# Linformer attention and a gated FFN: k' of batch 1 transposed by TensorE instead of by a DMA

## The chip, the cores and the metric

The kernel runs on one core of a Trainium2 chip. The metric is the device time of one execution in microseconds (us); of several runs the median is given. The core's engines are TensorE (PE in the profile; PEld are its weight loads), VectorE (DVE), ScalarE (ACT), GpSimd (POOL) and SyncE (SP). Each takes its instructions in the order in which the program issues them and waits on semaphores for the others. TensorE writes into PSUM, which has eight banks; VectorE and ScalarE read it from there.

## What is computed

Attention with projected keys and values (8 batches, 8 heads, 1024 positions, 64 features a head; E and F project the 1024 positions to 64), and behind it an FFN with a gelu:

```
k_proj = einsum('ks,bhsd->bhkd', E, k)
v_proj = einsum('ks,bhsd->bhkd', F, v)
scores = (q @ k_proj^T) / sqrt(64)
attn   = softmax(scores)
x      = attn @ v_proj            # to (8192 tokens, 512)
h      = x @ w_in                 # 512 -> 2048
out    = (h * sigmoid(1.702 h)) @ w_out   # 2048 -> 512
```

Below, k' and v' are `k_proj` and `v_proj`. For the scores, TensorE needs k' with the head's features on the partitions, that is, transposed from the form in which the projections leave it.

## The kernel before

**Blocks and slots.** The 8192 tokens are worked off in 16 blocks of 512, two to a batch. Block j needs its attention output `xT[j]`; then come the first FFN matmul (`ffn1`, L421) in slots 0 to 15, one slot for each 128 of the 2048 features (four matmuls with 512 columns and one gelu on ScalarE, L427 and L429), and the second FFN matmul. From block 1 on the second matmul is done in the manner of Strassen, as seven products named 1 to 7, each in two halves (L534), whose operands are sums of pieces of `gT` (the gelus' output) and of `w_out`, made by VectorE (`g_sum`, L508; `w_sums`, L465 and L469).

**What fills the slots.** The order of the instructions is written out by hand. `at(j, slot, ...)` puts further work behind a slot of block j, in the order of the calls; slots from O = 16 on are the halves of the seven products. In block 1 stand the following, all of them for the next batches:

- slot 1: SyncE's DMA transposes of the first half of q of batch 1 (`q_dma`, L264); slot 12: the second half
- slot 5: the projections of k and v of batch 1 (`proj`, L184), 16 matmuls into one PSUM bank, and `kv_out`: VectorE copies k' to `k_b` (L232), SyncE transposes it by DMA into `kts[1]` (L233), and VectorE copies v' into `vx1` and `vqs[1]` (L225, L226)
- slot 6: the last two operations of `w_sums` on VectorE
- slots 7, 13 and 15, ahead of what `at` puts there: the four sums of `g_sum` each, over four, three and one chunk of features
- slot O + 1, behind product 1: the scores of block 2 (`scores`, L274), which read `kts[1]` and the first half of q, and their exponentials on ScalarE (L293), for which ScalarE loads another table first; slots O + 3 and on: the values (`tok`, L399) and their transposes (`x_tr`, L414); slot O + 9: the scores of block 3

The k' of the other batches takes two ways. That of batch 0 is transposed by TensorE in three pieces: `k_piece` calls `k_tr` (L203), which transposes against an identity into PSUM (L207) and has VectorE copy the result into `kts[0]` (L209). That of batches 2 to 7 goes by DMA (L233 and L784).

**PSUM banks.** Each of the eight banks is one buffer: whoever takes it next waits until the last reader of the one before is done. Until the slots of block 1 end (`opening`), `f_tile` deals out banks 0 to 3 in turn, afterwards banks 0 to 4:

```
f_next[0] += 1
return bank(f_next[0] % (4 if opening[0] else 5), shape, dt)
```

In block 1 the projections of batch 1 are the 57th taker (bank 1), slots 6, 7 and 8 take banks 2, 3 and 0, slot 9 bank 1 again, slots 10 to 12 banks 2, 3 and 0. The scores, the values, the projections of batch 2 and the slots of block 2 go on with the count, now over five banks; slot 15 of block 2 is the 109th taker. From there the count is no longer used: the rest is a list of steps with banks named by hand (L598), which begins with the products of block 2 (L661), while scores and exponentials of the next blocks are mixed in (L741 and L740):

```
BANK = dict(FD=0, FB=4, FG=0, A0=6, A1=1, B0=7, B1=3, G0=2, G1=5, S10=5, S11=7, V00=4, V01=0,
            S00=3, S01=2, V10=6, V11=5, D0=2, D1=5, PJ=1)
AHEAD = {
    (2, None):
        "F1.0@2 F1.1@2 Fc1@2 sc.1@4 sc.0@4 ex.1.0@4 ex.1.1@4 F2.0@2 ex.0.0@4 ex.0.1@4 F2.1@2 sc.1@5 "
```

F1.0 and F1.1 are the halves of product 1 of block 2, into bank FD; Fc1 copies it on ScalarE into bank FB (L643); `sc` and `ex` are scores and exponentials.

Of the kernel before, what the change touches and what calls it, by code (L numbers as in the profile page):

```python
# [18 lines left out]
def kernel(ctx, tc, q, k, v, E, F,  # L19
                                                     moe_w_in, moe_w_out, out):  # L20
    nc = tc.nc
# [91 lines left out]
    kts = [consts.tile([P, HP, KP], BF16, name=f"kt{i}") for i in range(2)]  # L113
# [25 lines left out]
    def f_tile(shape, dt=F32):  # L139
        f_next[0] += 1  # L140
        return bank(f_next[0] % (4 if opening[0] else 5), shape, dt)
# [18 lines left out]
    for i, cp in enumerate((nc.vector.tensor_copy, nc.scalar.copy)):  # L160
        t_ps = f_tile([P, J // 2, 2 * KP], BF16)
# [10 lines left out]
    def eft(j, cols=slice(0, 2 * KP)):  # L172
        return efts[j // (J // 2)][:, j % (J // 2), cols]
# [4 lines left out]
    def proj(b):  # L178
        def go():
            if b not in kvps:  # L180
                kvps[b] = f_tile([P, H, D])
            for j in range(J):
                for e, r in enumerate((LO, HI)):
                    nc.tensor.matmul(kvps[b][r], eft(j, slice(e * KP, (e + 1) * KP)),  # L184
                                     (kt, vt)[e][b][:, :, j, :],
                                     start=(j == 0), stop=(j == J - 1))
        return go
# [8 lines left out]
    def k_piece(h0, n):  # L196
        k_ps = proj0(0, h0, n)
        k_b = att.tile([KP, n, D], BF16, name=f"k0_b{h0}", bufs=1)
        nc.vector.tensor_copy(k_b, k_ps[LO])
        warm(2)  # L200
        k_tr(k_b, h0 // 2)

    def k_tr(k_b, p0):  # L203
        n = k_b.shape[1] // 2
        t_ps = f_tile([P, n, KP], BF16)
        for p in range(n):
            nc.tensor.transpose(t_ps[:, p, :], k_b[:, 2 * p:2 * p + 2, :].rearrange("k t d -> k (t d)"),  # L207
                                ident[:KP, :KP])
        nc.vector.tensor_copy(kts[0][:, p0:p0 + n, :], t_ps)  # L209

    def vx_of(b, p):
        return vx1[:, 2 * p:2 * p + 2] if b == 1 else vx0[p]
# [7 lines left out]
    def v_out(b, v_ps):  # L220
        vv = v_ps[HI].rearrange("k (u x) d -> k u x d", x=4)
        for r, xs_ in ((LO, X_LO), (HI, X_HI)):
            if b == 1:
                vx = vx1[r, :, :D].rearrange("k (u x) d -> k u x d", x=4)
                nc.vector.tensor_copy(vx[:, :, xs_], vv[:, :, xs_])  # L225
            nc.vector.tensor_copy(vqs[b % 2][r].rearrange("k (u e) d -> k u e d", e=2), vv[:, :, xs_, :])  # L226

    def kv_out(b, cp=nc.vector.tensor_copy):
        def go():
            ps = kvps.pop(b)  # L230
            k_b = att.tile([KP, H, D], BF16, name="k_b")
            cp(k_b, ps[LO])  # L232
            nc.sync.dma_start_transpose(out=kts[b % 2], in_=k_b.rearrange("k h d -> k (h d)"))  # L233
            v_out(b, ps)
        return go

    q0s = [[early[:, (4 + 2 * g + u) * TB:(5 + 2 * g + u) * TB].rearrange("p (j i s) -> p j i s", j=2, i=2)
            for u in range(2)] for g in range(2)]
# [21 lines left out]
    def q_dma(b, j0=0, n=J):  # L260
        def go():
            if j0 == 0:
                qT[b] = att.tile([P, J, HP, P], BF16, name="qT")
            nc.sync.dma_start_transpose(out=qT[b][:, j0:j0 + n].rearrange("r j p s -> r (j p) s"),  # L264
                                        in_=qt[b][:, j0:j0 + n].rearrange("s j h d -> s (j h d)"))
        return go
# [542 lines left out]
    def at(j, slot, *fs):  # L809
        fill.setdefault((j, slot), []).extend(fs)  # L810
# [44 lines left out]
    for p in range(HP):  # L855
        at(0, Q + (4, 6, 9, 11)[p], tok(1, p, 0), tok(1, p, 1))
        at(0, Q + (6, 9, 11, 12)[p], x_tr(1, p, 0), x_tr(1, p, 1))
    at(1, 1, q_dma(1, 0, JB))
    at(1, 5, proj(1), kv_out(1))
    at(1, 12, q_dma(1, JB, JB))  # L860
    for u in range(2):
        at(1, O + 1, scores(2, u))
# [7 lines left out]
    at(1, O + 6, q_dma(2))  # L870
    at(2, 3, spread(3, nc.gpsimd), lambda: load(3))
    at(2, 1, proj(2), kv_out(2, nc.scalar.copy))
    for i, f in enumerate(w_in_sums()):
        at(2, (4, 6, 8, 10, 15, 15)[i], f)
# [49 lines left out]
    for j in range(2, 14):  # L924
        ahead(j, None)
        for word in STEPS:
            m = word.replace("-", "+-").split("+")
            name, n = m[0], j + int(m[1] if len(m) > 1 else 0)
# [3 lines left out]
    for word in END:  # L932
        name, n, swap, banks = re.fullmatch(r"(.*)@(\d+)(!?):?(.*)", word).groups()
# [32 lines left out]
```

## Time and profile before

| | |
|---|---|
| median of 3 runs | 476.46 us (476.27 to 476.97) |
| the profiled execution | 476.55 us, of it the span of the profile 474.7 us |
| TensorE busy | 464.2 us, 98% of the span |
| VectorE, ScalarE busy | 317.1 us, 320.1 us (67% each) |
| GpSimd busy | 83.2 us (18%) |
| TensorE's granted clock | 1.00 in every part of the span |
| slots 0 to 15 of block 1 | up to 68.68 us |
| scores of block 2 | from 72.46 us |
| products of block 2 | from 103.52 us |

The span is what the profile covers; the rest of the time lies before and behind it. A row of the timeline gives the start and the length in us, the engine, the line of the kernel, the operation, the tile written and the tile read, their sizes, how many instructions are taken together, and in brackets how long the engine stood idle before it and what ended that. In the chain of waits, followed back from the end of the program, each piece gives a start, a length and what it was; "SPq" is SyncE issuing transfers, "issue" the time in which nothing was waited for that the profile shows.

### The profile page before, as it was taken

To read this page: it belongs to the slowest core of one execution; us is meant where nothing else is said; L and a number is where in the kernel's file an instruction comes from. 1 tells how busy PE (TensorE), PEld (TensorE's weight loads), DVE (VectorE), ACT (ScalarE), POOL (GpSimd) and SP (SyncE) were. 2 spreads that over 40 slices of the span, in tenths; PEclk is the share of its full clock that TensorE was granted. 3 is DMA by queue.
4 is the path that set the end of the run, shared out by engine and by line. 5 is a ranking of instruction groups with operands and counts; after the bars stand their busy time and mean duration, and the time that the engine had idled before them with its cause. 6 is when DMAs were issued, how large, how long until landed. Compare 5 with 4: busy or idle time off the path is not lost.

```text
span 474.7 us, 10490 instructions
## 1 busy us (share of the span) xinstructions
PE 464.2 (98%) x4331; PEld 356.7 (75%) x4331; DVE 317.1 (67%) x589; ACT 320.1 (67%) x556; POOL 83.2 (18%) x104
## 2 busy tenths in 40 slices
PE   8999998998999999999999999999999999999996
PEld 4644446555778788787888878787888878888885
DVE  4503895399495775858587675867768585859472
ACT  2665455566596787967687886857788695848561
POOL 7562161062032100501041010500000000000000
PEclk9999999999999999999999999999999999999999
DMA  9999999979999999945999389942280413412022
GB/s 169 200 188 206 228 169 146 253 145 188 124 202 211 205 179 212 169 92 140 215 217 128 116 130 217 193 92 97 61 210 9 105 70 91 155 27 88 1 90 90
DMA packets 132963, 69.19 MB, mean 146 GB/s; under 512 B 98340, under 2 KB 122420, under 8 KB 132916
## 3 DMA queue, kind: packets, MB, share of 16 engines
q0 software_dynamic: 86816, 30.43, 58.1%
q1 hardware_dynamic: 46020, 37.84, 32.7%
q8 instruction: 34, 0.56, 0.5%
q10 hardware_dynamic: 80, 0.26, 0.2%
q14 instruction: 13, 0.11, 0.1%
HBM read 72.88 MB, written 16.99 MB: 189 GB/s over the span
## 4 chain that ended last, share of the span: by engine, by line
PE 81%; DMA 13%; DVE 2%; POOL 1%; SPq 1%; ACT 1%; issue 1%; DVEq 0%; POOLq 0%; ACTq 0%
PE k_ps L661 35%; PE k_ps L712 34%; DMA q_sb<-in_q_dram 4%; PE k_ps L274 3%; PE k_ps L427 3%; DMA w_in_sb<-in_moe_w_in_dram 2%; PE k_ps L184 2%; DMA w_out_sb<-in_moe_w_out_dram 2%; PE k_ps L534 2%; DMA v_sb<-in_v_dram 2%; DMA kt<-k_b 2%; SPq L264 1%; PE k_ps L754 1%; DVE xT L748 1%; POOL k_sb L59 0%
## 5 line engine op out<-in xcount | busy, mean ns | idle before, releaser
L646 DVE TENSOR_TENSOR q_even<-k_ps,q_even 128x512 f32<-128x512 f32 x104 | 70.3, 688 | 55.2 <-PE k_ps L712 54.0
L661 PEld LDWEIGHTS <-sg 128*128 128x128 bf16 x896 | 87.3, 98 | 11.8 <-issue 1.8
L712 PEld LDWEIGHTS <-late 128*128 128x128 bf16 x832 | 80.4, 98 | 12.7 <-PE k_ps L661 2.3
L712 PE MATMUL k_ps<-xw,late 128*128 128x256 bf16 x624 | 89.3, 273 | 0.6 <-DVE xw L500 0.6
L661 PE MATMUL k_ps<-tw,sg 128*128 128x256 bf16 x672 | 82.5, 273 | 0.3 <-DVE u_sb L643 0.3
L728 ACT ACTIVATE gT<-k_ps 128x512 bf16<-128x512 f32 x104 | 62.3, 600 | 27.0 <-PE k_ps L712 25.4
L661 PEld LDWEIGHTS <-gT 128*128 128x128 bf16 x672 | 65.8, 98 | 8.3 <-issue 0.4
L712 PEld LDWEIGHTS <-w_in_sb 128*128 128x128 bf16 x624 | 58.3, 98 | 17.7 <-issue 10.8
L728 ACT ACTIVATE gT<-q_even 128x512 bf16<-128x512 f32 x104 | 61.4, 630 | 4.4 <-DVE q_even L646 4.3
L712 PE MATMUL k_ps<-xT,w_in_sb 128*128 128x256 bf16 x416 | 62.3, 273 | 1.0 <-ACT vq L643 1.0
L643 ACT COPY q_even<-k_ps 128x512 f32<-128x512 f32 x63 | 36.0, 590 | 38.8 <-PE k_ps L712 38.0
L71 POOL DMA_DIRECT2D q_sb<-in_q_dram x48 | 42.1, 904 | 105.3 <-DMA qT<-q_sb 68.6
L661 PE MATMUL k_ps<-w_out_sb,gT 128*128 128x256 bf16 x448 | 55.6, 273 | 0.1
L427 PE MATMUL k_ps<-xT,w_in_sb 128*128 128x512 bf16 (+1 forms) x200 | 42.7, 371 | 0.0
L508 DVE TENSOR_TENSOR sg<-gT 128x1024 bf16<-128x1024 bf16 (+2 forms) x64 | 41.4, 647 | 0.0
L429 ACT ACTIVATE gT<-k_ps 128x512 bf16<-128x512 f32 (+1 forms) x50 | 28.9, 580 | 17.9 <-PE k_ps L427 17.7
L427 PEld LDWEIGHTS <-w_in_sb 128*128 128x128 bf16 x200 | 19.3, 98 | 21.3 <-issue 0.8
L748 DVE TENSOR_TENSOR xT<-k_ps,rbc 128x512 bf16<-128x512 f32 x52 | 33.5, 679 | 0.0
L643 DVE COPY q_even<-k_ps 128x512 f32<-128x512 f32 x41 | 27.1, 684 | 8.7 <-PE k_ps L712 8.7
L716 ACT COPY k_ps<-k_ps 128x512 f32<-128x512 f32 x52 | 29.3, 588 | 3.2 <-DVE xT L748 1.2
L712 PE MATMUL k_ps<-xw,w_in_sb 128*128 128x256 bf16 x208 | 31.2, 273 | 0.0
L712 PE MATMUL k_ps<-xT,late 128*128 128x256 bf16 x208 | 31.0, 273 | 0.0
(134 smaller groups left out, 541.0 us busy)
## 6 DMA issues: line engine op xcount, KB each, us to landing
out_dram<-o_sb SPq DMA_DIRECT2D x31, 512.0 KB
rbc<-rdr SPq DMA_DIRECT2D x24, 512.0 KB
k_sb<-in_k_dram POOLq DMA_DIRECT2D x7, 1024.0 KB, 10.4
v_sb<-in_v_dram POOLq DMA_DIRECT2D x7, 1024.0 KB, 16.2
q_sb<-in_q_dram POOLq DMA_DIRECT2D x48, 128.0 KB, 6.0
w_in_sb<-in_moe_w_in_dram POOLq DMA_DIRECT2D x8, 256.0 KB, 11.4
w_out_sb<-in_moe_w_out_dram POOLq DMA_DIRECT2D x4, 512.0 KB, 11.5
q_even<-in_q_dram POOLq DMA_DIRECT2D x12, 128.0 KB, 14.8
```

Source lines behind the costliest of these rows:

```text
L71: nc.gpsimd.dma_start(out=qt[b][:, j], in_=qv[:, j])
L274: nc.tensor.matmul(outs[i][r.start + c:r.start + c + w], lhsTs[i][ri, c:c + w], rhss[i][ri], start=True, stop=True)
L427: nc.tensor.matmul(h_ps, w_in_sb[:, kc, fc * P:(fc + 1) * P], xT[j][:, kc, ts], start=(kc == 0), stop=(kc == KC - 1))
L429: nc.scalar.activation(gts[j][:, fc, ts], h_ps, AF.Gelu_apprx_sigmoid)
L508: nc.vector.tensor_tensor(t[i - 1], in0, in1, op=ALU.add if i == 1 else ALU.subtract)
L643: (nc.scalar.copy if (n in ON_ACT) != swap else nc.vector.tensor_copy)(out_, in_)
L646: nc.vector.tensor_tensor(out_, in0, in1, op=ALU.add)
L661: nc.tensor.matmul(at_(n)[:, 0 if one else t], x[:, c, t * P:(t + 1) * P], w[:, c], start=(i in (1, 5) and (one or t == 0) and c == 0), st ...
L712: nc.tensor.matmul(at_(h)[:, r], a[:, c, f:f + P], w[:, c], start=(i in (1, 5) and r == 0 and c == 0), stop=(i in (2, 3, 4) and r == 1 and ...
L716: nc.scalar.copy(new(f"B{m}", [P, 2, TH], f"B{n}"), at_(f"A{n}"))
L728: nc.scalar.activation(out_, in_, AF.Gelu_apprx_sigmoid)
L748: nc.vector.tensor_tensor(x_of(j)[:, u, :], at_(f"V{p[1]}{t}"), rbc[j][:, u, :], op=ALU.mult)
```

## The change

k' of batch 1 is no longer transposed by SyncE's DMA but by TensorE. `kv_out` keeps `k_b` of batch 1 in a list in place of issuing the DMA transpose; `k_tr` is given the batch, and is called behind slot 8 of block 1, three features' chunks behind the projections. It takes one bank of the ring, issues four transposes on TensorE and one copy of 128x256 on VectorE into `kts[1]`. The k' of batch 0 and of batches 2 to 7 goes as before.

```diff
-    def k_tr(k_b, p0):
+    def k_tr(k_b, p0, b=0):
         n = k_b.shape[1] // 2
         t_ps = f_tile([P, n, KP], BF16)
         for p in range(n):
             nc.tensor.transpose(t_ps[:, p, :], k_b[:, 2 * p:2 * p + 2, :].rearrange("k t d -> k (t d)"),
                                 ident[:KP, :KP])
-        nc.vector.tensor_copy(kts[0][:, p0:p0 + n, :], t_ps)
+        nc.vector.tensor_copy(kts[b][:, p0:p0 + n, :], t_ps)
...
             k_b = att.tile([KP, H, D], BF16, name="k_b")
             cp(k_b, ps[LO])
-            nc.sync.dma_start_transpose(out=kts[b % 2], in_=k_b.rearrange("k h d -> k (h d)"))
+            if b == 1:
+                k_bs.append(k_b)
+            else:
+                nc.sync.dma_start_transpose(out=kts[b % 2], in_=k_b.rearrange("k h d -> k (h d)"))
             v_out(b, ps)
         return go
+
+    k_bs = []
...
     at(1, 5, proj(1), kv_out(1))
+    at(1, 8, lambda: k_tr(k_bs[0], 0, 1))
     at(1, 12, q_dma(1, JB, JB))
```

## The prediction

> **What bounds the kernel now.** I read the page first, then the chain of waits in order of time around the change, then the timeline there engine by engine, last the waits of the later stretches. TensorE is busy for 98% of the span; time can only be won or lost where it stands still. From 116 us on it is busy for 352.46 of 354 us, and no transfer is in the chain after 72.46 us. What is gained or lost at 60 to 75 us, where this change lies, therefore reaches the end unless something between 75 and 116 us swallows it.
>
> The chain of waits there (start, us, what):
>
> ```profile
> 63.15 9.27 DMA kt<-k_b
> 72.42 0.04 issue
> 72.46 0.62 PE k_ps L274 x16
> 73.08 1.85 PE k_ps L534 x16
> 74.94 0.23 PE k_ps L399 x4
> ```
>
> k' of batch 1 is ready in SBUF at 60.85 us, but SyncE issues the transposes of q's first half until 63.10, and the transposed k' lands 9.27 us after its own issue begins. TensorE has finished the part before (L534) at 70.81 us and stands for 1.65 us until the scores (L274) may start. That is all that the change can remove.
>
> The timeline of VectorE in the same place, with the one TensorE weight load that had to wait, and below it four rows of ScalarE (start, us, engine, line; in brackets the idle time before and what ended it):
>
> ```profile
> 60.17 0.68 DVE L232 CAST k_b<-k_ps 64x512 bf16<-64x512 f32 x1 [2.83 <-PE k_ps L184]
> ...
> 62.02 0.42 DVE L226 CAST vq<-k_ps 64x256 bf16<-64x256 f32 x1
> 62.47 2.29 DVE L465 TENSOR_TENSOR tw<-w_out_sb,rbc 128x2048 bf16<-128x2048 bf16 x1
> 62.49 0.68 PEld L427 LDWEIGHTS <-w_in_sb 128*128 128x128 bf16 x4 [0.18 <-DVE vq L226]
> 64.68 1.22 DVE L469 CAST tw<-rbc 128x2048 bf16<-128x2048 f32 x1
> 65.81 0.68 DVE L508 TENSOR_TENSOR sg<-gT 128x1024 bf16<-128x1024 bf16 x1
> ...
> 67.74 0.68 DVE L508 TENSOR_TENSOR sg<-gT,sg 128x1024 bf16<-128x1024 bf16 x1
> 68.34 0.55 DVE L508 TENSOR_TENSOR sg<-gT 128x768 bf16<-128x768 bf16 x1
> 67.22 0.60 ACT L429 ACTIVATE gT<-k_ps 128x512 bf16<-128x512 f32 x1 [0.33 <-PE k_ps L427]
> 70.89 0.57 ACT L565 COPY k_ps<-k_ps 128x512 f32<-128x512 f32 x1 [1.35 <-PE k_ps L534]
> 71.48 1.28 ACT L293 ACT_TABLE_LOAD   x1
> 72.91 0.60 ACT L293 ACTIVATE expT<-k_ps 128x512 bf16<-128x512 f32 x1
> ```
>
> Two things are to be seen. VectorE has no gap from 60.17 to 71.35 us. And the weight load at 62.49, the first of slot 9, waited for vq (L226), the last reader of the projections' bank: four PSUM banks go round in this stage, and slot 9 is the fourth taker after the projections.
>
> **The change, part by part.**
>
> *Removed:* one transpose issue on SyncE (1.30 us at 63.15) and its 9.27 us in flight, and with them TensorE's 1.65 us. On SyncE the second half of q's transposes is next (issued 64.61 to 72.36); it could begin up to 1.5 us earlier if its q has landed. Its readers, the scores of block 3, start at 81.68 and waited for VectorE, not for it: nothing.
>
> *Added on TensorE:* four transposes 64x128 to 128x64 behind slot 8. The same operation for batch 0 (L207) has 199 ns each by its own record; a pair there holds the next weight load up from 9.68 to 9.84, 0.08 us each. Four cost 0.32 us by that (0.16 at half, 0.80 at full records). Their inputs are there: k_b since 60.85, and the bank, which is now the projections' own, since 62.44, just as slot 9 had it.
>
> *Added on VectorE:* one copy 128x256 bf16 out of PSUM. L415 copies exactly that in 282 ns (278 to 292).
>
> *The new wait.* The transposes' result takes the fourth turn of the ring, where slot 9 was. Slots 9, 10 and 11 take the other three; slot 12 comes round to the transposes' bank and must wait until VectorE has copied it. VectorE's order is the program's: behind the projections' copies stand the two w_out sums put at slot 6 (L465 2.29, L469 1.22) and the four gT sums of slot 7 (L508), and only then the copy of slot 8. So the copy starts where now the slot-13 sum starts, 68.34, and ends at 68.62; 0.05 us later, as from vq to the load at 62.49, slot 12 starts at 68.67. Bounds of this: 68.55 if the copy overlaps its predecessor more, 68.85 if it waits for the 68.42 end and takes 0.35.
>
> Before, slots 12 to 15 (16 matmuls of 0.216) ended at 68.68, so slot 12 began at 65.22. **It is 3.45 us late** (3.3 to 3.65). In the new kernel TensorE would have come to slot 12 at 62.64 + 0.32 + 3 x 0.865 = 65.55, so it idles 3.1 us there, and the four transposes cost nothing: this wait hides them. By the Trainium skill, "TensorE: Matmul & The Clock Gate", Part 4, a transpose takes some 390 ns alone for 128x128; four such would put TensorE at 66.8 in place of 65.55, still before 68.67, and the sum would be the same.
>
> Behind slot 12 on TensorE's queue stand slots 13 to 15, part 1 of the second matmul and the scores. VectorE's later gT sums wait for their gelu and move along: the slot-13 sum starts at 71.4 (its gelu, 67.22 + 0.60, plus 3.45), the slot-15 sums end at 74.4; what part 5 reads of them is done by 73.7, and part 5 starts at 74.9. Nothing.
>
> *What is won back.* Part 1 ends at 70.81 + 3.45 = 74.26. k' (68.62) and the first half of q are there, so the scores follow at once. But ScalarE's path then ends last: from the end of part 1 it takes 0.08 to L565, 0.57 for it, 0.02, 1.28 for the table load, 0.02, 0.60 for the first exponential and some 0.04 to TensorE, 2.61 in all, against 0.03 + 0.62 + 1.85 = 2.50 on TensorE. The values (L399) start at 74.26 + 2.61 = 76.87 in place of 74.94. Of the 1.65 us, 1.5 are won.
>
> That makes + 3.45 - 1.52 = + 1.93 us (1.75 to 2.2) at 77 us.
>
> *A second wait, from the count of banks.* The transposes take one turn more of the ring, and every later turn falls one bank further. Within the ring this changes nothing, for the distances stay. (Where four banks become five, the scores meet the bank of block 1's slot 15, whose gelu ends at 73.0, before 74.26.) But block 2 goes over from the ring to banks named by hand. Its slot 15 is the 109th taker: 109 mod 5 is bank 4, and bank 0 is slot 11's. With one more it is the 110th: bank 0, the bank named FD, into which the very next TensorE work, product 1 of block 2 (L661), writes. So that must wait until slot 15's gelu has been read out of it:
>
> ```profile
> 103.55 0.60 ACT L429 ACTIVATE gT<-k_ps 128x512 bf16<-128x512 f32 x1 [0.27 <-PE k_ps L427]
> 105.34 0.57 ACT L643 COPY k_ps<-k_ps 128x512 f32<-128x512 f32 x1 [1.19 <-PE k_ps L661]
> ...
> 111.16 0.69 DVE L643 COPY u_sb<-k_ps 128x512 f32<-128x512 f32 x1 [0.47 <-PE k_ps L661]
> ```
>
> Slot 15's gelu ends at 104.15; the chain has L661 begin at 103.52. With 0.05 to TensorE it begins at 104.20: **0.68 us late** (0.63 by the release alone; 0.85 if the weight load, now fetched ahead at 103.14, is paid as well). Nothing covers it: the copy at 105.34 waits for L661, and behind it on ScalarE stand the table load and the exponentials that the chain follows up to 111 us. The other named banks (4, 3, 2 and 1) fall to slots 14, 13, 12 and 11, whose gelus are done before they are needed.
>
> *Does it last?* VectorE's run of work from 94.81 on hangs on a gather issued by SyncE behind q's transposes of batch 2, which wait for a load; it may stay in place while TensorE is later. But at 111.16 VectorE was already waiting 0.47 us for TensorE, so a later TensorE only lengthens that: nothing is swallowed.
>
> **Sum:** + 1.93 + 0.68 = **+ 2.6 us** (2.35 to 3.05). Profiled execution: span 474.7, 476.55 in all; with the change 479.15. The median of the runs lies 0.09 below it: 476.46 + 2.6 = **479.1**.
>
> **The rivals.**
>
> *A, the copy holds nobody up (not slower).* If slot 12 found its bank free, part 1 would end at 70.81 + 0.32 and the values start at 71.13 + 2.61 = 73.74, 1.2 us earlier; with 0.68 lost at 103.5, 0.5 is left, and VectorE's 0.47 us of waiting at 111.16 lets through no more if its work from 94.81 on stays where it is: 476.0. For it: for batch 0 the copies (L209) follow their transposes within 0.3 us. Against: VectorE is idle before those, and full here. It decides if the copy gets past the sums. Chance 0.04.
>
> *B, the change frees nothing: q is the late one.* The first half of q's transposes shares SyncE's queue with k', and the scores could be waiting for it all along; with a free slot 12 the time would be 476.5 + 0.7 = 477.1. Against: the chain names k', issued after it, and in my forecast TensorE comes at 74.26, after both. 0.04.
>
> *C, one of the waits is missing or is partly swallowed.* TensorE idles 0.89 us in 103 to 116; if that closed, or if the second wait did not come about, 0.7 to 0.9 less: 478.2 to 478.4. For it: much there hangs on VectorE, busy for 12.46 of those 13 us. Against: its waits follow TensorE's own work. 0.10.
>
> *D, the clock drops in the gap.* TensorE's longest gap in mid-kernel is now 1.65 us, and the granted clock is 1.00 in every stretch; the new gap is 3.1 us. The records do show a slower TensorE: at 5.04, 5.46 and 5.89 us the loads of the 128x512 warm matmuls follow each other in 0.43 us, where later ones take 0.216. Were the 16 matmuls of slots 12 to 15 run so, 16 x 0.21 = 3.4 more: 482.5; half of them, 480.8. It decides from the point at which a gap is long enough to count. 0.10. The same page of the skill, Part 1, has the clock halved after an idle window of some 3.4 us; by that length 3.1 us is just too short and the sum stays, and no row here shows such a gap yet. Its closing table warns of gaps above about 3 us, and by that D would be the case.
>
> **How the numbers follow.** Forecast 0.72, its own range 478.6 to 479.8 (the sum's bounds, and 0.3 us of spread: the runs before lie from 476.27 to 476.97). A to D take 0.28. The range 478.0 to 480.8 takes in C and D's lower half; it leaves out A, B, D's upper half and some of the tails, under 2 in 10. A measurement of this kernel can tell 0.2%, 0.95 us, from no change: faster is under 475.5 (a tail of A, 0.02), same up to 477.4 (A, B: 0.07), slower the rest, 0.91.
>
> **What would show it.** Right: slot 12's weight load idle some 3 us with VectorE's new copy (line 209) as releaser; that copy starting at about 68.3, straight after the fourth L508; no wait of L274 for a transfer; the values at 76.9; L661 waiting some 0.6 us for ScalarE's gelu at about 106. Wrong: the copy near 63 us (A); L274 waiting for qT (B); no wait of L661 for the gelu, or less lateness at 116 us than at 106 (C); matmuls of 0.4 us after the gap (D).

## The result, and the profile after

The changed kernel takes 481.41 us (median of 4 runs, 479.85 to 483.79) against 476.50 us before: a ratio of 1.0106, 95% interval 1.0064 to 1.0148. It is slower, as forecast, but by 4.9 us where 2.6 were forecast, and outside the range. The profiled execution took 481.41 us, with a span of 479.6 us.

Line numbers from L234 on are higher by five in the changed kernel (L427 is L432, L508 L513, L534 L539, L661 L666, L274 L279), and by six in some of the experiments from their own edit on.

The place of the first wait, from the timelines of VectorE and TensorE in the changed kernel:

```profile
68.00 0.68 DVE L513 TENSOR_TENSOR sg<-gT,sg 128x1024 bf16<-128x1024 bf16 x1
68.72 0.29 DVE L209 COPY kt<-k_ps 128x256 bf16<-128x256 bf16 x1
73.32 0.56 DVE L513 TENSOR_TENSOR sg<-gT 128x768 bf16<-128x768 bf16 x1 [4.32 <-ACT gT L434]
62.99 0.29 PE L207 MATMUL k_ps<-ident,k_b 64*128 64x64 bf16 x4
63.21 2.76 PE L432 MATMUL k_ps<-xT,w_in_sb 128*128 128x512 bf16 x12
69.06 5.30 PE L432 MATMUL k_ps<-xT,w_in_sb 128*128 128x512 bf16 x16 [3.09 <-DVE kt L209]
```

The copy of k' comes straight after the fourth gT sum, and slot 12 waits 3.09 us for it. What had not been put into the sum stands in the last row: the 16 matmuls of slots 12 to 15 take 5.30 us in place of the 3.46 (16 x 0.216) of the kernel before. The windows of the changed kernel show a lower clock there (the stretch, its length, busy time of PE, PEld, DVE, ACT and POOL with their instructions, then the granted clock, the DMA share and GB/s):

```profile
66.00:69.00 3.00, 0.00 (x0) 0.00 (x0) 2.93 (x6) 0.60 (x1) 2.39 (x3) 1.00 1.15 169
69.00:72.00 3.00, 2.94 (x8) 1.04 (x8) 0.01 (x1) 0.60 (x1) 0.00 (x0) 0.52 1.28 182
72.00:75.00 3.00, 3.00 (x17) 1.58 (x16) 1.64 (x4) 1.74 (x3) 0.89 (x1) 0.91 2.00 128
```

In the three us after the gap only eight matmuls ran, at a granted clock of 0.52. Before the change that clock is 1.00 throughout.

The place of the second wait, in the chain of waits of the kernel before and then of the changed one:

```profile
91.32 12.19 PE k_ps L427 x56
103.52 1.76 PE k_ps L661 x16
```

```profile
107.73 0.61 ACT gT L434
108.34 0.04 issue
108.38 1.92 PE k_ps L666 x16
110.30 0.03 ACTq L648
```

Product 1 of block 2 now follows slot 15's gelu; before, it followed slot 15's matmuls. The lateness against the kernel before changes from stage to stage as follows (starts in us, from the chains and timelines of the two profiled executions; slot 12 before is 68.68 less 16 matmuls of 0.216):

| | before | after | later by |
|---|---|---|---|
| copy of k' to `k_b`, ahead of all that was changed | 60.17 | 60.43 | 0.26 |
| slot 12 | 65.22 | 69.06 | 3.84 |
| ScalarE's copy behind part 1 (L565, L570) | 70.89 | 76.40 | 5.51 |
| values (L399, L404) | 74.94 | 78.94 | 4.00 |
| second part behind them (L534, L539) | 75.16 | 79.34 | 4.18 |
| product 1 of block 2 (L661, L666) | 103.52 | 108.38 | 4.86 |
| ScalarE's copy behind it (L643, L648) | 105.34 | 110.37 | 5.03 |
| end of the span | 474.7 | 479.6 | 4.9 |

The first 0.26 us is the opening, the work ahead of all that was changed. This copy of k' starts at 60.17 in the one profile of the kernel before and at 60.38 to 61.02 in the twelve others of this case; whether the change has a part in that isn't shown. The rest is: first wait + 3.58, slow matmuls + 1.67, won back at the scores - 1.51, second wait + 0.68, and twice a group behind a wait that takes longer, the values + 0.18 (0.40 us in place of 0.23 in the chain) and product 1 + 0.17 (1.92 in place of 1.76). This longer time behind a wait is called the refilling of TensorE's pipeline below; the name is a reading, the times are measured. (The chain of the changed kernel names VectorE's sums ahead of ScalarE's copy L570. The copy starts at 76.40, 0.08 us after part 1 ends on TensorE, at 76.32; before, it was 70.89 after 70.81, the same 0.08. So it still follows TensorE.)

### The profile page after: what moved, and what is told of

Read it like the earlier page. It is cut to its first block, busy times and chain, and to the rows that moved or that the text cites. A ratio compares the mean times of both kernels' runs of the same rounds, so it can differ in the third digit from the quotient of the medians.

```text
span 479.6 us, 10488 instructions
## 1 busy us (share of the span) xinstructions
PE 465.5 (97%) x4327; PEld 356.7 (74%) x4335; DVE 317.8 (66%) x590; ACT 319.9 (67%) x556; POOL 83.2 (17%) x104
## 4 chain that ended last, share of the span: by engine, by line
PE 89%; DVE 4%; DMA 3%; ACT 2%; POOL 1%; issue 1%; DVEq 0%; ACTq 0%; POOLq 0%
PE k_ps L666 35%; PE k_ps L717 34%; PE k_ps L432 8%; PE k_ps L279 3%; PE k_ps L444 3%; PE k_ps L184 3%; DMA v_sb<-in_v_dram 3%; PE k_ps L539 2%; DVE sg L513 1%; PE k_ps L759 1%; DVE xT L753 1%; DVE tw L470 0%; POOL k_sb L59 0%; POOL v_sb L59 0%; PE k_ps L404 0%
## 5 line engine op out<-in xcount | busy, mean ns | idle before, releaser
L666 PEld LDWEIGHTS <-sg 128*128 128x128 bf16 x896 | 87.3, 98 | 11.8 <-issue 1.8
L666 PE MATMUL k_ps<-tw,sg 128*128 128x256 bf16 x672 | 82.5, 273 | 0.3 <-DVE u_sb L648 0.3
L666 PEld LDWEIGHTS <-gT 128*128 128x128 bf16 x672 | 65.7, 98 | 9.2 <-issue 1.4
L648 ACT COPY q_even<-k_ps 128x512 f32<-128x512 f32 x63 | 36.0, 590 | 38.9 <-PE k_ps L717 38.1
L666 PE MATMUL k_ps<-w_out_sb,gT 128*128 128x256 bf16 x448 | 55.6, 273 | 0.8 <-ACT gT L434 0.7
L432 PE MATMUL k_ps<-xT,w_in_sb 128*128 128x512 bf16 (+1 forms) x195 | 44.4, 381 | 3.4 <-DVE kt L209 3.1
L513 DVE TENSOR_TENSOR sg<-gT 128x1024 bf16<-128x1024 bf16 (+2 forms) x64 | 41.5, 648 | 6.1 <-ACT gT L434 6.1
L432 PEld LDWEIGHTS <-w_in_sb 128*128 128x128 bf16 x200 | 19.6, 100 | 25.7 <-issue 6.4
L648 DVE COPY q_even<-k_ps 128x512 f32<-128x512 f32 x41 | 27.1, 685 | 8.7 <-PE k_ps L717 8.7
```

What stands on the lines that cost most here:

```text
L432: nc.tensor.matmul(h_ps, w_in_sb[:, kc, fc * P:(fc + 1) * P], xT[j][:, kc, ts], start=(kc == 0), stop=(kc == KC - 1))
L513: nc.vector.tensor_tensor(t[i - 1], in0, in1, op=ALU.add if i == 1 else ALU.subtract)
L648: (nc.scalar.copy if (n in ON_ACT) != swap else nc.vector.tensor_copy)(out_, in_)
L666: nc.tensor.matmul(at_(n)[:, 0 if one else t], x[:, c, t * P:(t + 1) * P], w[:, c], start=(i in (1, 5) and (one or t == 0) and c == 0), st ...
```

## The experiments

The theory: two waits on banks, each of the size above, and on top of them a clock that drops in the 3.1 us gap in most executions. Against it stood that the slow matmuls have another cause, that the second wait is hidden, and that the transposes on TensorE cost by themselves.

**Work in the gap.**

```diff
     at(1, 8, lambda: k_tr(k_bs[0], 0, 1))
+    at(1, 11, lambda: warm(14))
```

> The changed kernel with 14 matmuls of zeros (128x512, 0.216 us each, into a bank that is free) behind slot 11, so that TensorE works through most of the 3.1 us in which it waits for VectorE's copy of k'. Theory 'bank waits and clock' (3.1 us of idleness lower the clock, the 16 matmuls of slots 12 to 15 then take 5.35 us in place of 3.46): the clock stays at 1.00 in every execution, slots 12 to 15 take 3.5 us, and the time is 476.5 + 2.3 (first wait, net) + 0.84 (second wait) = 479.6, all runs within 0.5 us of each other. Rival 'the slow matmuls have another cause' (refilling of TensorE's queue, the transfers running at that time): slots 12 to 15 still take over 5 us and the time is some 481.4.

479.93 us (six runs, 479.85 to 480.18; ratio 1.0058, 1.0039 to 1.0077). Its timeline of TensorE:

```profile
66.25 3.19 PE L152 MATMUL k_ps<-zeros 128*128 128x512 bf16 x14
69.50 3.61 PE L432 MATMUL k_ps<-xT,w_in_sb 128*128 128x512 bf16 x15
```

Slots 12 to 15 start just as late after the transposes as in the changed kernel (6.06 us against 6.07), but they take 3.61 us in place of 5.30 (one record is missing of the 16), at a clock of 0.998 or more in every run. TensorE did 14 matmuls more and the kernel became 1.5 us faster. The loss behind the gap is the clock, and the gap's idleness is its cause: only the idleness was taken away, and the loss went with it.

**The result in a bank outside the ring,** which takes both waits away and leaves the change otherwise as it is:

```diff
-        t_ps = f_tile([P, n, KP], BF16)
+        t_ps = (x_any if b else f_tile)([P, n, KP], BF16)
```

> The changed kernel with the transposes' result put into a bank outside the ring (bank 7, which has no other user until product 5 of block 1). Theory 'bank waits and clock': VectorE's copy stays where it is, at about 68.7, but nobody on TensorE waits for it; slot 12 starts at once, no clock drop, no wait of L666 for the gelu at 104; the scores follow part 1 at 71.1 and the values start at 73.8, 1.2 us earlier than before the change. By VectorE's 0.47 us of waiting at 111 us only that much is left at the end: 476.0 (475.3 if all of it passes). Rival 'q is the late one': the scores wait for q's transposes at 72.4 and the time is 476.5 or more. Rival 'transposes on TensorE cost more than 0.3 us': 476.5 to 477.5.

> The changed kernel with the transposes' result in a bank outside the ring, once more, beside the next one: 476.0, 0.5 to 0.8 below the kernel before the change.

476.00 us (12 runs; before, on the same chip, 476.67; ratio 0.9983, 0.9971 to 0.9996), and the second time 475.85 (before 476.46; ratio 0.9995, 0.9983 to 1.0008). There is no wait for k' and none for the gelu, and the scores follow part 1 at once, as these rows of TensorE show:

```profile
63.22 6.22 PE L432 MATMUL k_ps<-xT,w_in_sb 128*128 128x512 bf16 x28
71.33 0.62 PE L279 MATMUL k_ps<-qT,kt 64*32 64x512 bf16 x16
74.01 0.40 PE L404 MATMUL k_ps<-vx,expT 128*128 128x130 bf16 x4 [0.21 <-ACT expT L298]
```

So rival B of the prediction, by which the scores wait for q, is out. The time is the 476.0 of rival A, but that is a coincidence: A had the second wait in it, and this kernel has none. In the chain of the first of these runs the stretch from 88.7 to 111 us no longer goes through TensorE:

```profile
88.74 1.82 SPq L269
90.56 0.05 issue
90.61 0.58 SPq L547
91.19 0.05 issue
91.24 0.02 SPq L328
91.26 0.04 issue
91.29 3.52 DMA rc<-den
94.81 0.02 issue
94.83 0.07 DVE rc L337
...
109.58 1.09 DVE late L496
110.67 0.08 issue
110.75 0.05 DVE u_sb L648
```

The gather waits on SyncE behind the transposes of q of batch 2, which stand where they stood, and VectorE's work behind it ends at 110.67, as before. So of the 1.2 us that the change is worth at the values (74.01 against 74.94, with an opening 0.26 us later), 0.6 to 0.7 came to the end by the medians; the interval of the second ratio takes in 1.

**The same, with the ring's count put forward by one,** so that the second wait alone is there:

```diff
             opening[0] = False
+            f_next[0] += 1
```

> As the run with the bank outside the ring, but with the ring's count put forward by one behind block 1, as in the changed kernel, so that slot 15 of block 2 takes bank 0 again. Theory 'bank waits and clock': L666 waits for slot 15's gelu as in the changed kernel (0.7 us idle and 0.16 for filling TensorE's pipeline again); the time is 0.84 above the run without it if that passes in full, 0.4 above it if VectorE's backlog had eaten the gain already. Rival 'the second wait is hidden': equal times.

476.88 us (12 runs; ratio to before 0.9999, 0.9987 to 1.0010), 0.88 above the run without the count on the same chip. The list of TensorE's waits (us in total, times, longest) has the one for the gelu again:

```profile
PE k_ps L666 <- ACT gT L434: 0.7, 1, 0.7
```

The second wait passes in full, and it alone takes away all that the change had to give. This, not the kernel without the count, is the case of rival A, and A had 476.0 for it. It carried the whole 1.2 us on to product 1; of them 0.87 are left there (102.91 without the count, 103.52 before, the opening taken off), and the second wait takes 0.68 and 0.17 more for the refilled pipeline.

**The changed kernel with only the second wait taken away:**

```diff
             opening[0] = False
+            f_next[0] += 4
```

> The changed kernel with the ring's count put forward by four more behind block 1, so that block 2 has the banks of the kernel before the change; the first wait stays. Theory 'bank waits and clock': no wait of L666 for the gelu; the time is 0.84 below the changed kernel's: 480.6 where the clock drops (a granted clock of 0.5 for 3.4 us or less), 479.0 where it doesn't, and so a spread of one to two us between the runs as the changed kernel has it. Rival 'the second wait is hidden': 481.4.

480.65 us (six runs, 479.03 to 482.05; ratio 1.0076, 1.0053 to 1.0099), 0.76 below the changed kernel. Among executions with the same clock it is 0.8 below (table further down): 479.03 against 479.84 and 479.85 at full clock, 480.61 against 481.45 by the medians of the middle group. The wait for the gelu is gone, the one for k' is there. Its profiled execution, the slowest of the six:

```profile
69.39 6.45 PE L432 MATMUL k_ps<-xT,w_in_sb 128*128 128x512 bf16 x16 [3.08 <-DVE kt L209]
```

The same gap as in the changed kernel, and all 16 matmuls slow.

**A shorter and a longer gap.** The first puts one of VectorE's sums behind the copy, the second does it twice more ahead of the copy:

```diff
-        at(*((0, Q + 10), (0, Q + 13), (0, Q + 13), (0, Q + 13), (1, 6), (1, 6))[i], f)
+        at(*((0, Q + 10), (0, Q + 13), (0, Q + 13), (0, Q + 13), (1, 6), (1, 9))[i], f)
```

```diff
+    at(1, 8, w_sums[5], w_sums[5])
     at(1, 8, lambda: k_tr(k_bs[0], 0, 1))
```

> The changed kernel with one of VectorE's two w_out sums of slot 6 (L474, 1.22 us) put behind slot 9 and so behind the copy of k'; the copy starts 1.13 us earlier and TensorE's gap is about 1.9 us in place of 3.1. Theory 'bank waits and clock', with a length of gap from which the clock drops: the gap is too short, the granted clock stays at 1.00 in every execution; 476.5 + 2.3 - 1.15 (first wait, net) + 0.84 (second wait) = 478.5, all runs within 0.7 us. Rival 'any gap of TensorE lowers the clock': 479.5 to 481.

> The changed kernel with the last w_out sum (L474, 1.13 us apart) done twice more on VectorE ahead of the copy of k', so that TensorE's gap is about 5.4 us in place of 3.1; nothing else is changed in what is computed. Theory 'bank waits and clock': the clock drops in every execution, none is left at 1.00; without the clock 476.5 + 2.3 + 2.3 + 0.84 = 481.9, with it 1.5 to 3.4 us more: 483.4 to 485.3. Rival 'the clock drops by chance, whatever the gap': a part of the runs at 481.9.

Short: 478.81 us (seven runs, 478.50 to 479.99; ratio 1.0034, 1.0017 to 1.0051), the clock at 0.999 or 1.000 in all seven; the spread was twice what was expected, by one run, and not by the clock. Long: 484.82 us (five runs, 483.83 to 484.86; ratio 1.0156, 1.0136 to 1.0175), the clock at 0.992 to 0.995 in all five. The rows of TensorE, the short one first:

```profile
68.00 3.61 PE L432 MATMUL k_ps<-xT,w_in_sb 128*128 128x512 bf16 x16 [1.95 <-DVE kt L209]
```

```profile
71.45 6.18 PE L432 MATMUL k_ps<-xT,w_in_sb 128*128 128x512 bf16 x16 [5.48 <-DVE kt L209]
```

A gap of 1.95 us lowered the clock in none of seven runs, one of 5.48 us in all five.

**The copy on ScalarE,** with the bank left in the ring:

```diff
-        nc.vector.tensor_copy(kts[b][:, p0:p0 + n, :], t_ps)
+        (nc.scalar.copy if b else nc.vector.tensor_copy)(kts[b][:, p0:p0 + n, :], t_ps)
```

> The changed kernel with the copy of the transposed k' on ScalarE in place of VectorE; the bank stays in the ring. Theory 'bank waits and clock': ScalarE copies at about 63.5, slot 12 doesn't wait, and there is no gap and no clock drop; the second wait stays, since the ring's count is the changed kernel's: as the run with the bank outside the ring and the count put forward, 476.9. Rival 'a turn of the ring among the slots costs by itself, whoever copies': a wait of L432 remains and the time is over 477.5.

476.88 us (12 runs, 476.44 to 478.65, all at a clock of 0.999 or 1.000; ratio 1.0005, 0.9990 to 1.0019). Five of the twelve lie above 477.6 without a lower clock; on the same chip the kernel before has four runs at 478.4 to 478.8 with a clock of 0.999 or 1.000 as well. What this second spread is, no run shows. In its timeline of ScalarE:

```profile
62.68 1.08 ACT L434 ACTIVATE gT<-k_ps 128x512 bf16<-128x512 f32 x2 [0.65 <-PE k_ps L432]
63.65 0.38 ACT L209 COPY kt<-k_ps 128x256 bf16<-128x256 bf16 x1
64.40 0.60 ACT L434 ACTIVATE gT<-k_ps 128x512 bf16<-128x512 f32 x1 [0.38 <-PE k_ps L432]
```

The copy fits between two gelus, and slot 12 doesn't wait. A turn of the ring among these slots costs nothing by itself; the first wait came from VectorE's queue alone. The second wait is there (0.7 us), and the time is that of the run with the bank outside the ring and the count put forward.

**q's transposes behind the gather,** on top of the bank outside the ring, against what held back the rest there:

```diff
-    at(1, O + 6, q_dma(2))
+    at(1, O + 11, q_dma(2))
```

> The kernel with the transposes' result in a bank outside the ring, and besides q's transposes of batch 2 put from behind product 5 (slot O + 6) to behind the gather of block 3's sums (slot O + 11) on SyncE's queue. That run's chain goes from the end of q's transposes' issue on SyncE (90.6) over the gather (94.8) to VectorE, which works without a gap until 110.7 and holds back the rest. Theory 'VectorE's backlog behind SyncE holds back the rest of the gain': the reciprocal starts at some 92.5 in place of 94.8, VectorE is through before TensorE needs it, and the 0.7 us that were lost between 75 and 111 us come through: 475.3. Rival 'the rest is held back elsewhere', or the later transposes of q or k' of batch 2 become a wait at the scores of block 4: 476.0 or more.

> The same with q's transposes of batch 2 behind the gather, on the same chip as the run beside it. Theory 'VectorE's backlog behind SyncE holds back the rest': 0.3 us below the run beside it, as the trace of this kernel has it when its opening, which came 0.6 us later there, is taken off. Rival 'the rest is held back elsewhere': equal.

The first time 476.31 us (before 476.84; ratio 0.9982, 0.9967 to 0.9998), not the 475.3 expected. The cause that was named is gone, for the reciprocal starts 2.1 us earlier and VectorE then waits for gelus of TensorE's results again:

```profile
92.74 0.35 DVE L337 RECIPROCAL rc<-rc 128x32 f32<-128x32 f32 x1
93.01 2.29 DVE L492 TENSOR_TENSOR late<-w_in_sb 128x2048 bf16<-128x2048 bf16 x2
97.11 0.69 DVE L513 TENSOR_TENSOR sg<-gT 128x1024 bf16<-128x1024 bf16 x1 [1.81 <-ACT gT L434]
```

But this execution had its k' transposes at 63.59 us, the one it is to be compared with at 63.00: the opening took back more than the 0.3 us that were won. Side by side on one chip, the second time, it took 475.70 us (11 runs, 475.56 to 476.20; ratio to before 0.9991, 0.9981 to 1.0000) against 475.85 (12 runs, 475.36 to 477.01). The difference has the expected sign and is too small for these medians to settle. In the traces it is there twice: from the copy of k' to `k_b` to the last 64 matmuls of the chain it is 402.86 and 402.85 us with q's transposes late, 403.20 and 403.09 without, and 403.87 before the change. So they give back 0.2 to 0.3 us.

**The changed kernel once more.**

> The changed kernel itself, to see how its executions spread. Theory 'bank waits and clock', with a clock that goes low for whole periods (of some 3.4 us by the granted clock of the traces) or not at all: the runs fall into groups by their mean granted clock, about 479.8 at 1.00, 481.4 at 0.995 or 0.996, 483 at 0.993, and most are not at 1.00. Rival 'the spread is the transfers': no relation of time and clock.

481.52 us (six runs, 479.84 to 482.79; ratio 1.011, 1.009 to 1.013). All executions of the two kernels that have the 3.1 us gap, by their mean granted clock:

| mean granted clock | changed kernel (10 runs) | without the second wait (6 runs) |
|---|---|---|
| 0.999, 1.000 | 479.84, 479.85 | 479.03 |
| 0.995, 0.996 | 481.28, 481.41, 481.41, 481.49, 481.54, 481.61 | 480.47, 480.61, 480.69 |
| 0.993 | 482.79, 483.79 | 481.86, 482.05 |

The middle group lies 1.4 to 1.8 us above the first, the last 1.2 to 2.5 us above the middle one. In 13 of 16 executions the gap lowered the clock; of the 84 runs of the experiments without a gap of over 1.95 us, none had a clock under 0.998.

## Why the prediction was right in direction and wrong in size

- *TensorE's 1.65 us and the ScalarE path that takes over:* right. 1.52 us were to be won back at the values, 1.51 were; the values wait 0.21 us for the first exponential.
- *The transposes cost nothing here:* right. They add 0.22 us in front of slot 9 (62.99 to 63.21), all of it inside the gap; where the gap is gone, the kernel is not slower than before for them.
- *The first wait:* right in place and mechanism, 3.58 us for 3.45. The sum had the copy overlap its predecessor, as VectorE's sums do among themselves; it didn't, but began at 68.72, 0.04 us after that one's end. The bound of 3.65 holds it.
- *The second wait:* right, 0.68 us for 0.68. The refilling costs 0.17 us more, which only the upper bound of 0.85 had; together that is what was measured. The same 0.18 us at the values, which now wait too, were not in the sum at all.
- *Does it last:* right. The last 64 matmuls of the chain start 5.02 us late (469.06 against 464.04), as late as ScalarE's copy behind product 1.
- *Rival A:* its case did not come, and its price was 0.9 us too low, as the runs with the second wait alone show (476.88 for 476.0).
- *D, the clock drops in the gap (0.10):* **the step that failed.** The prediction saw the gap of 3.1 us rightly and put nothing into the sum for the clock behind it. The drop came in 13 of 16 executions. D's row, 0.43 us a matmul, and the cost that it reckoned, 1.7 us for half of the 16 matmuls and 3.4 for all, were about right: + 1.67 us in the profiled execution, and up to about 3 where all 16 are slow (482.05 against 479.03). Only its chance of 0.10 was wrong, and no row spoke for so low a one: the trace had a gap of 1.65 us without a drop, the slow matmuls of the start, and nothing between. The Trainium skill ("TensorE: Matmul & The Clock Gate") had both answers: Part 1 has an idle window of some 3.4 us, by which the sum stood, and the closing table warns of gaps above about 3 us. The closing table agrees with the runs; Part 1, taken as a bound for a single gap, does not.

Taken together: forecast + 2.6; + 0.13 for the copy, + 0.35 for the pipeline, + 0.26 for the opening and + 1.67 for the clock give 5.0; 4.9 were measured, between the medians and between the two profiled executions. The executions in which the clock did not drop, 479.84 and 479.85, are inside the range of 478.0 to 480.8.

## What to carry to other kernels

When a piece of work moves to another engine, ask first which buffer it borrows and which queue its last reader stands in: the four transposes and the copy cost nothing here, the turn of the bank ring that they took cost 3.6 us at one place and 0.85 at another. At the first a reader far back in VectorE's queue held the bank; at the second, banks named by hand followed a count that had moved by one. A gap on TensorE of about three us is to be priced with the clock that it may lose as well, about 1.6 us here and in some executions twice that. The cheap repair here was a bank that nobody else wanted at that time.

## What the runs showed of the hardware that was not expected

The clock goes low for whole periods. In stretches of half a microsecond, the edges reckoned from the mixed ones, the granted clock is 0.50 from about 69.1 to 72.5 us in the changed kernel's profile and, for twice as long, from 68.35 to 75.2 in the one without the second wait and from 69.85 to 76.7 in the one with the long gap: 3.4, 6.8 and 6.8 us. The Trainium skill has a window of 3413 ns that runs free of the kernel ("TensorE: Matmul & The Clock Gate", Part 1), and these lengths agree with one and two of it. So do the mean clocks: half the clock for 3.4 of 480 us makes 0.996, for 6.8 us 0.993.

How long it stays low goes with where it falls. In the changed kernel's profile the clock fell 0.1 us after TensorE had begun again, and stayed low for 3.4 us. In the two others it fell while TensorE still stood, 1.0 and 1.6 us before it began again, and in the repeat of the changed kernel 0.9 us before; in all three it stayed low for 6.8 us. That the rest of the gap spoils the next window too would fit; four profiles are all there is for it.

It does not take a window in which TensorE stands still from end to end. In the kernel without the second wait TensorE's last matmul before the gap ended at 66.31 us and the clock was low from 68.35, 2.0 us later; a gap of 1.95 us never did it in seven runs. The rows of that kernel where TensorE stops, where the clock falls and where it comes back (the clock is the third number from the end):

```profile
66.00:66.50 0.50, 0.31 (x2) 0.03 (x1) 0.50 (x2) 0.17 (x2) 0.50 (x1) 1.00 1.09 119
68.00:68.50 0.50, 0.00 (x0) 0.00 (x0) 0.50 (x2) 0.00 (x0) 0.50 (x1) 0.85 1.25 200
75.00:75.50 0.50, 0.50 (x4) 0.17 (x3) 0.50 (x2) 0.31 (x1) 0.00 (x0) 0.82 0.23 12
```

That some 2 us of idleness within one window are enough would fit both, and also that 3 of 16 executions escaped, in which a window's edge would have cut the 3.1 us into two short halves; this was only argued, no run moved the edge.

Left open: four of 47 runs of the kernel before, beside the first eight experiments, also had a clock of 0.995 or 0.996 and took 478.8 to 479.2 us; beside the last three, two of 23 had 0.992 and 0.989 and took 485.0 and 486.1 us. No profile of such a run was taken, and the kernel's one profile has no gap over 1.65 us. So the clock can also drop without the gap, though in 6 of 70 runs and not in 13 of 16. The column of the granted clock doesn't show every slow stretch either: it has 1.00 for the first 6 us of the kernel before, where the loads of the 128x512 matmuls follow each other in 0.43 us.
